# One order list for the whole kernel: the head's loads, transposes and key products move into the program's words

## The chip, the cores and the metric

The kernel runs on one NeuronCore of a Trainium2 chip. Four engines compute: PE (TensorE, matrix products), DVE (VectorE), ACT (ScalarE) and POOL (GpSimd). SP (SyncE) only issues transfers (DMAs); ACT and POOL can issue them too. Each engine works through its own queue in order, and all DMAs are carried out by the same 16 DMA engines. The metric is the device time of one execution in microseconds (us).

## The reference

Tokens S = 2048, width D = 640, 32 attention heads of 20, FFN width 1728, all tensors in bf16.

```
xn  = layernorm(x)                                  # per token, no gain
q,k,v = split(xn @ wqkv)                            # 640 -> 3 x 640
phi(t) = where(t > 0, t + 1, exp(t)) + 1e-6
kv  = sum_s phi(k)_s v_s^T   per head;  z = sum_s phi(k)_s
s   = ((phi(q) @ kv) / (phi(q) . z + 1e-6)) @ wo    # linear attention
g   = silu(relu(xn @ w1) @ w2)                      # FFN, 640 -> 1728 -> 640
out = x + s * g
```

## The kernel before

Tokens are cut into 16 tiles of 128; a tile of x is 128 x 640 bf16, 160 KB. The weights for the keys (wk) are loaded in pieces of 128 rows, 160 KB each; the first FFN weight (w1) in seven column pieces, 320 KB each (the last, piece 6, 240 KB). Most large products use Strassen-like units of seven products each (`unit`, L1159, and `seven`, L1022): the operand sums that they need are made on DVE (L975).

**Recording and order.** Each operation is recorded with what it reads and writes (`Sched`); waits follow from that. `place` then sets the order on each engine from estimated costs. For PE and SP the order is always that of the recording; for ACT, DVE and POOL it is that of the recording up to the call of `end_of_head`, and after it a choice among the next 60 operations of the engine by due times. The recording after the head is driven by a list of words, `PROGRAM`, one word for a step (`a0.s5`: step 5 of unit a0; `n8`: normalise tile 8; `Kb8`: one half of the keys of tile 8).

**The head**, the part that the change touches, was written out as calls in the function body:

- Loads. On the ACT queue x1, x2, x3. On the SP queue x0, wk piece 0, wk piece 1, wk piece 2, wk pieces 3 and 4 in one DMA, w1 pieces 2 and 5, x4, x5, w1 piece 6, x6, x7, w1 pieces 0 and 3 (`x_load` L540, `wk_load` L564, `w1_load` L560).
- Tiles 0 to 3 take a short way to the keys, since their full statistics come late: half of the mean by `bn` on DVE (L635), half or all of it by `mean_act` on ACT (L666), `centre` on DVE (L680, L676), five transposes on PE (L687), copies of the transposed tile out of PSUM by DVE (L697) or ACT (L699), then the key products `K_mm` (L714) in parts by wk piece. `fill` (L603) is a row of products with no use but to keep PE busy: 32 before the first transposes, 3 after those of tile 0. The scale 1/sigma comes later from `aggr` (DVE L639, POOL L641 and L643) and is applied in `K_evac` (ACT L724), which gives exp and relu of the keys.
- Five FFN blocks of the first 512 tokens (`H_block`, PE L804, relu on ACT L808), columns 4, 5, 10, 11, 12, need w1 pieces 2, 2, 5, 5, 6.
- Tiles 4 to 7: statistics on DVE (`LN_stats`), the normalised tile (`LN_norm`, DVE L654), a transposing DMA on the SP queue (L703), then `K_tile` (ten products at L714, and exp and relu). Tiles 0 to 3 are normalised and transposed the same way for later use. `K_fin` (DVE L740, L742) ends the keys of a tile.

After the head come FFN and q products (L1203, L766), the products of keys with x (L1030, L1501), the denominators (L921, L934), and from about 110 us on the FFN's second product and the output (L1030, L1835). The last tile's last 320 columns leave in two pieces (`s_last`), cut by `LC`; each piece has five products (L1835), a product with the gate on DVE, the addition of x on DVE (both L975), and a DMA (L1878).

## Time and profile before

| what | us |
|---|---|
| median of 3 runs (lowest, highest) | 202.2 (202.18, 202.8) |
| span of the profiled execution, first to last instruction | 201.4 |
| PE busy in it | 197.8 |
| DVE busy | 175.1 |
| ACT busy | 130.9 |
| POOL busy | 37.9 |

The span is 0.8 us under the median: the runs' time takes in what lies before the first and after the last instruction, and no time of the profiled execution other than its span was kept. "Busy" is the time in which an instruction of the engine was under way; products on PE overlap, and their ends are modelled. In the rows of the trace a row that merges several instructions gives its start, its length, and in brackets how long the engine had been idle before it and what released it. "PEld" is the loading of a product's stationary operand, "SPq" and "ACTq" are the queues while they issue a DMA.

### The profile page before, as it was taken

The numbers are of one execution on the slowest core, as the hardware profiler recorded it, in microseconds if no ns is written. First come the engines' busy times: TensorE is split into PE (matmuls) and PEld (weight loads), VectorE is DVE, ScalarE is ACT, GpSimd is POOL, SyncE is SP. The second block draws the span as 40 slices with busy tenths as digits, with TensorE's granted clock in tenths as the row PEclk, the third lists the DMA queues.
The fourth block names the chain that finished last, engine by engine and source line by source line (L and its number), as shares of the span: only waits on it lengthen the run. The fifth ranks groups of instructions, "written<-read, shape, count | busy, mean of one in ns | idle before, by whom it ended". The sixth has DMA issues, their size and how long they took to land.

```text
span 201.4 us, 3693 instructions
## 1 busy us (share of the span) xinstructions
PE 197.8 (98%) x1340; PEld 122.6 (61%) x1340; DVE 175.1 (87%) x413; ACT 130.9 (65%) x273; POOL 37.9 (19%) x66
## 2 busy tenths in 40 slices
PE   8999999999999999999999999999999999999995
PEld 7655644455455454445654777777777777767773
DVE  5988999999999888999975999999779786985674
ACT  6598957998999999978653224371555555445643
POOL 3174060363134654152200000000000000000000
PEclk9999999999999999999999999999999999999999
DMA  6977974765545896575910987865961244012103
GB/s 196 326 211 120 264 174 30 189 164 119 116 92 107 163 260 131 102 142 104 245 34 2 324 217 207 263 201 145 373 232 65 68 163 165 0 67 68 65 33 98
DMA packets 38471, 30.43 MB, mean 151 GB/s; under 512 B 13749, under 2 KB 38453, under 8 KB 38453
## 3 DMA queue, kind: packets, MB, share of 16 engines
q1 hardware_dynamic: 32581, 23.28, 41.2%
q0 software_dynamic: 4624, 5.57, 14.3%
q10 hardware_dynamic: 1248, 1.35, 2.1%
q8 instruction: 10, 0.16, 0.3%
q14 instruction: 8, 0.07, 0.1%
HBM read 15.81 MB, written 5.24 MB: 105 GB/s over the span
## 4 chain that ended last, share of the span: by engine, by line
PE 95%; DMA 3%; SPq 1%; DVE 0%; issue 0%; DVEq 0%
PE psT L1030 43%; PE psT L1203 31%; PE psT L714 8%; PE psT L804 5%; DMA reg<-in_A_wqkv_dram 3%; PE psT L1501 2%; PE psT L1835 1%; PE psT L822 1%; PE psT L766 1%; PE psT L1626 1%; PE psT L1600 1%; PE psT L934 1%; DVE reg L975 0%; SPq L564 0%; SPq L540 0%
## 5 line engine op out<-in xcount | busy, mean ns | idle before, releaser
L1203 PE MATMUL psT<-reg 128*128 128x512 bf16 (+2 forms) x159 | 41.7, 370 | 0.0
L1030 PE MATMUL psT<-reg,regH 128*128 128x320 bf16 (+1 forms) x224 | 34.8, 299 | 0.0
L1030 PE MATMUL psT<-reg 128*128 128x320 bf16 (+1 forms) x178 | 29.4, 299 | 0.0
L1030 PEld LDWEIGHTS psT<-reg,regH 128*128 128x128 bf16 (+1 forms) x224 | 21.8, 98 | 8.7 <-DVE psT L975 0.2
L1203 PEld LDWEIGHTS psT<-reg 128*128 128x128 bf16 (+1 forms) x159 | 15.5, 98 | 16.1 <-DVE reg L975 0.7
L902 POOL DMA_DIRECT2D regH<-reg x16 | 18.4, 1238 | 27.0 <-DMA regH<-reg 9.4
L1037 ACT ACTIVATE reg<-psT 128x320 f32<-128x320 f32 (+1 forms) x24 | 10.4, 435 | 17.4 <-PE psT L1030 15.9
L1030 PEld LDWEIGHTS psT<-reg 128*128 128x128 f16 (+1 forms) x178 | 17.3, 98 | 7.2 <-DVE regH L1256 0.4
L975 DVE TENSOR_TENSOR reg<-reg 128x1024 f16<-128x1024 bf16 (+10 forms) x30 | 18.9, 645 | 0.7 <-PE psT L1203 0.6
L1253 ACT ACTIVATE regH<-psT 128x512 bf16<-128x512 f32 (+1 forms) x24 | 14.6, 607 | 4.1 <-PE psT L1203 3.9
L975 DVE TENSOR_TENSOR psT<-psT,reg 128x320 f32<-128x320 f32 (+1 forms) x22 | 11.9, 542 | 5.6 <-PE psT L1030 5.1
L1030 PE MATMUL psT<-reg,pqT 128*128 128x320 bf16 (+1 forms) x84 | 16.3, 299 | 0.0
L1662 ACT ACTIVATE wv_sb<-psT 128x320 bf16<-128x320 f32 (+1 forms) x22 | 9.2, 423 | 10.3 <-PE psT L1030 9.9
L635 DVE BATCH_NORM_STATS2 stats<-reg 128x6 f32<-128x320 bf16 x32 | 13.9, 475 | 1.9 <-DMA reg<-in_A_x_dram 1.9
L1850 ACT ACTIVATE reg<-psT 128x640 bf16<-128x640 f32 (+1 forms) x14 | 8.0, 570 | 9.2 <-PE psT L1030 9.2
L714 PE MATMUL psT<-reg 128*128 128x320 bf16 x80 | 12.3, 299 | 0.0
L1037 ACT ACTIVATE psT<-psT 128x320 f32<-128x320 f32 x17 | 7.3, 427 | 6.8 <-PE psT L1030 6.8
L975 DVE TENSOR_TENSOR reg<-psT,reg 128x320 f32<-128x320 f32 (+2 forms) x19 | 9.5, 504 | 1.4 <-PE psT L1030 1.3
L781 ACT ACTIVATE regE<-psT 128x512 bf16<-128x512 f32 x16 | 9.6, 607 | 1.1 <-PE psT L766 0.5
L714 PEld LDWEIGHTS psT<-reg 128*128 128x128 bf16 x80 | 7.8, 98 | 4.3 <-ACT regH L808 0.3
L643 POOL TENSOR_TENSOR rsy<-rsv,mhalf 128x1 f32<-128x1 f32 x16 | 10.0, 622 | 1.3
L1030 PEld LDWEIGHTS psT<-reg,pqT 128*128 128x128 bf16 (+1 forms) x84 | 8.2, 98 | 3.2
(170 smaller groups left out, 397.9 us busy)
## 6 DMA issues: line engine op xcount, KB each, us to landing
regH<-reg POOLq DMA_DIRECT2D x16, 320.0 KB, 3.7
reg<-in_B_w_dram SPq DMA_DIRECT2D x12, 320.0 KB, 4.6
scr<-rden SPq DMA_DIRECT2D x4, 640.0 KB, 6.7
reg<-in_A_x_dram SPq DMA_DIRECT2D x4, 640.0 KB, 6.3
out_dram<-reg SPq DMA_DIRECT2D x14, 160.0 KB, 1.8
regE<-scr SPq DMA_DIRECT2D x3, 640.0 KB, 5.3
reg<-in_A_x_dram SPq DMA_DIRECT2D x4, 320.0 KB, 3.8
reg<-in_A_wo_dram SPq DMA_DIRECT2D x6, 160.0 KB, 5.0
```

What stands on the lines that cost most here:

```text
L635: sc.op("DVE", lambda eng: eng.bn_stats(stats[:, t, a, :], xv[:, HN * a:HN * (a + 1)]), R=[("xin", xs(t))], W=[("stats", t, a)])
L643: sc.op("POOL", lambda eng: eng.tensor_tensor(out=rsy[:, t:t + 1], in0=rsv[:, t:t + 1], in1=mhalf[:, :], op=ALU.pow), R=[("rsv", t), ("mha ...
L714: fns.append(lambda eng, a=a, k=k, lhs=lhs: eng.matmul(ps[bk[a]][:, 0:HN], lhsT=lhs, rhs=wk[:, k, HN * a:HN * (a + 1)], start=(k == 0), st ...
L781: exps.append(sc.op("ACT", lambda eng: eng.activation(out=e_, in_=src, func=ACTF.Exp), R=[key], W=[("er_e", es)]))
L804: sc.group("PE", [(lambda eng, k=k: eng.matmul(ps[b], lhsT=w1_col(k, P * f, P), rhs=src[:, k, :], start=(k == 0), stop=(k == C - 1))) for ...
L902: dma("POOL", lambda eng: eng.dma_start(zacc[a], src, **kw), R=[key] + after, W=[("zacc", a)], chain=zchain[a])
L975: sc.op("DVE", lambda eng: eng.tensor_tensor(out=out, in0=in0, in1=in1, op=op), R=R, W=W, extra=extra)
L1030: sc.group("PE", [(lambda eng, k=k, lhs=lhs, rhs=rhs: eng.matmul(ps[b][:, 0:HN], lhsT=lhs, rhs=rhs, start=(start and k == 0), stop=(k == n ...
L1037: sc.op("ACT", lambda eng: eng.activation(out=dst, in_=ps[b][:, 0:HN], func=ACTF.Copy), R=[("ps", b)], W=[dkey], extra=extra)
L1203: sc.group("PE", [(lambda eng, k=k, lhs=lhs, rhs=rhs: eng.matmul(ps[b][:, 0:nn], lhsT=lhs if tile is None else rhs, rhs=rhs if tile is Non ...
L1253: sc.op("ACT", lambda eng: eng.activation(out=dst, in_=ps[b], func=ACTF.Relu), R=[("ps", b)], W=[("hT", j, f)], extra=ex)
L1662: sc.op("ACT", lambda eng, lo=lo, hi=hi: eng.activation(out=g[:, lo:hi], in_=src[:, lo - HN * n:hi - HN * n], func=ACTF.Silu), R=[key, ("s ...
```

## The change

The calls of the head are deleted from the function body. `PROGRAM` gets a first part, ending at the word `|`, which says the head in words, so that one list sets the order of everything. What differs from the old head:

- x3 is loaded on the SP queue, no longer on ACT's. wk piece 1 is asked for ahead of piece 0, x3 follows piece 0, and pieces 3 and 4 are two DMAs with x5 between them. x4 stands between w1 pieces 2 and 5, x6 after piece 6, and x7 is the last load, behind w1 pieces 0 and 3.
- On PE the three idle products stay behind the transposes of tile 0, and the transposes of tile 1 come ahead of the first key product. Key products are cut by single wk pieces.
- Copies out of PSUM: the second part of tile 0 goes to ACT, and for tile 2 the parts change engines (DVE now makes four copies, ACT four; before five and three). On DVE the second half of tile 0's statistics stands ahead of the centring of tile 2.
- On ACT the evacuations of the keys of tiles 0 to 3 are interleaved differently, the last pair behind two FFN blocks' relu. The FFN blocks come in the order 4, 10, 5, 12, 11.
- Tiles 0 to 3 are normalised in the order 1, 0 (ahead of the keys of tile 4), 2, 3 (behind those of tile 7).
- The rest of `PROGRAM` holds the same words as before in another order in many places; it starts with block 11 in place of 10.
- `LC` goes from 160 to 192: the last two pieces are 192 and 128 columns wide in place of 160 and 160.

The diff, cut (the new functions only look after which PSUM bank is in use, and call the functions that were called before):

```diff
 PROGRAM = """
-H110 H112 H14 H111 T0 H15 SQ SK xa Q14 a0.s1 a0.s5 Q04 a0.s6 p1.s5 p1.s1 n8 wa xb a0.s2 a0.s7 p1.s6 rb a0.s3 a0.s4
...
+ax1 lx0 ba0 lk12 mh0 lk01 lx3 ax2 ma0 ce0 lk23 lk34 ma1 lx5 lk45 lw2 lx4 lw5 lw6 lx6 ce1 ma2 lw0
+lw3 tr0 pf3 cd0 tr1 cd2 ca1 bb0 lx7 k001 k012 ce2 k102 ca3 ba3 ba2 mh3 ma3 tr2 k123 k023 cd5 ca4 ce3 ag0
+k201 k212 k223 ba1 tr3 k034 cd6 k045 ca7 bb1 k134 k145 k234 ag1 ke0 bb2 kr0 ke1 k245 k301 k312 k324 ag2 S4
+bb3 ke2 k345 kr1 ag3 kr2 P4 P10 ke3 kr3 S5 P5 N4 P12 S6 N5 S7 N6 F0 N7 lx8 F2 lq P11
+F1 F3 N1 N0 KT4 F4 KT5 N2 SH0_1 F5 KT6 KT7 N3 S8 F6 SH0_2 |
+H111 H14 xa F7 H110 H112 SQ Q14 n8 T0 H15 a0.s1 SH0_3 a0.s5 SH0_4 Q04 a0.s6 p1.s5 p1.s1 a0.s2 wa a0.s7 p1.s6 xb
...
-    x_load(0)
-    x_load(1, 1, "ACT")
-    wk_load(0, 1)
-    x_load(2, 1, "ACT")
-    wk_load(1, 2)
-    x_load(3, 1, "ACT")
-    wk_load(2, 3)
-    wk_load(3, 5)
-    w1_load(2, 3, "SP")
-    w1_load(5, 6, "SP")
-    x_load(4)
-    x_load(5)
-    w1_load(6, NW, "SP")
-    x_load(6)
-    x_load(7)
-    for d in (0, 3):
-        w1_load(d, d + 1, "SP")
...
-    bn(0, 0)
-    mean_act(0, HN)
-    half_mean_dve(0)
-    centre(0)
-    mean_act(1, 0)
-    transposes(0, 0)
-    xcT_copy(0, 0, 0, "DVE")
-    centre(1)
-    fill(3)
-    K_mm(0, 2, 0, 1)
-    transposes(1, 6)
-    xcT_copy(0, 0, 1, "DVE")
-    mean_act(2, 0)
-    xcT_copy(1, 6, 0, "DVE")
-    xcT_copy(1, 6, 1, "ACT")
-    K_mm(0, 2, 1, KA)
-    K_mm(1, 4, 0, KA)
-    centre(2)
-    transposes(2, 0)
-    K_mm(0, 2, 2, 3)
...
+    def head_key(t, q, k0, k1):
+        b = (2, 4, 6, 0)[t]
+        assert bank[b] is None if k0 == 0 else bank[b] == ("K", t, k0)
+        bank[b] = bank[b + 1] = ("K", t, k1)
+        K_mm(t, b, k0, k1)
+
+    def head_copy(n, E):
+        t, part = n // 2, n % 2
+        b = (0, 6, 0, 0)[t]
+        assert bank[b + part] == ("T", t, part)
+        xcT_copy(t, b, part, E)
+        bank[b + part] = None
...
-    LC = [0, 160, 320]
+    LC = [0, 192, 320]
...
+        "lx": x_load,
+        "ax": lambda t: x_load(t, 1, "ACT"),
+        "lw": lambda d: w1_load(d, d + 1, "SP"),
+        "ba": lambda t: bn(t, 0),
+        "bb": lambda t: bn(t, 1),
+        "mh": half_mean_dve,
+        "ce": centre,
+        "tr": head_turn,
+        "cd": lambda n: head_copy(n, "DVE"),
+        "ca": lambda n: head_copy(n, "ACT"),
+        "pf": fill,
+        "ag": aggr,
+        "ke": head_exp,
+        "kr": head_relu,
+        "P": head_block,
+        "KT": K_tile,
+        "S": S, "N": N, "F": F,
```

The words read so: `lk12` loads wk piece 1 (rows from 1 up to 2), `k102` makes the key products of tile 1 with wk pieces 0 and 1, `cd5` copies part 1 of tile 2 on DVE (number = 2 x tile + part), `ca4` part 0 of tile 2 on ACT, `ma`, `mh`, `ba`, `bb` are the mean and statistics pieces, `S`, `N`, `F` are `LN_stats`, `LN_norm`, `K_fin`.

More of the change, by code (lines that the diff above doesn't have):

```diff
@@ L1365, in bass_recurrent_scan__linear_attn_block__dense_activation_relu__prompt_kernel, with head_turn, head_exp, head_relu @@
     HP = (4, 5, 10, 11, 12)
-    def K_tile(t, b):
+    bank = [None] * 8
+    copied = set()
+    def head_key(t, q, k0, k1):
[3 more added lines that the diff above has]
+        K_mm(t, b, k0, k1)
+    def head_turn(t):
+        b = (0, 6, 0, 0)[t]
+        for part in range(2):
+            assert bank[b + part] is None
+            bank[b + part] = ("T", t, part)
+        transposes(t, b)
+    def head_copy(n, E):
+        t, part = n // 2, n % 2
+        b = (0, 6, 0, 0)[t]
+        assert bank[b + part] == ("T", t, part)
+        xcT_copy(t, b, part, E)
+        bank[b + part] = None
+    def head_exp(t):
+        b = (2, 4, 6, 0)[t]
+        assert bank[b] == ("K", t, C)
+        K_exp(t, b)
+    def head_relu(t):
+        b = (2, 4, 6, 0)[t]
+        assert bank[b] == ("K", t, C)
+        K_relu(t, b)
+        bank[b] = bank[b + 1] = None
+    def head_block(f):
+        b = RB[ring[0] % len(RB)]
+        assert bank[b] is None
+        H_block(0, f)
+    def K_tile(t):
+        b = 2 * t - 8
+        assert bank[b] is None and bank[b + 1] is None
         K_mm(t, b)
```

83 lines of the change are left out of this document (31 added, 52 removed).

## The prediction

> **What bounds the kernel now.** I read the page first (span, engines, slices), then the chain that ended last, then the head's timeline, then the landings of single DMAs.
>
> ```profile
> span 201.4 us, 3693 instructions
> ...
> PE 197.8 (98%) x1340; PEld 122.6 (61%) x1340; DVE 175.1 (87%) x413; ACT 130.9 (65%) x273; POOL 37.9 (19%) x66
> ...
> PE   8999999999999999999999999999999999999995
> ```
>
> PE is busy all the time but in the first and the last of 40 slices. The chain, in order of time (start, length, what), shows where its row begins:
>
> ```profile
> 2.19 5.20 DMA reg<-in_A_wqkv_dram
> ...
> 7.43 1.53 PE psT L714 x10
> ...
> 9.24 2.99 PE psT L714 x22
> ...
> 17.62 5.47 PE psT L714 x40
> ...
> 132.56 54.22 PE psT L1030 x399
> ...
> 198.33 0.36 PE psT L1835 x5
> ```
>
> From 7.43 to 198.69 us the chain never leaves PE, and its lengths are those of products back to back: 399 products of 128x320 take 54.22 us, 136 ns each, and the 22 at 9.24 take 2.99, 136 ns each too. So the time is 7.43 us until PE's row begins, a fixed sum of products, and 2.7 us behind it. The change adds and removes no product. It can win only what lies ahead of 7.43 or behind 198.7; in between it can only lose.
>
> What PE does until 7.43, with the DVE and ACT work that feeds it:
>
> ```profile
> 4.10 0.64 DVE L680 TENSOR_SCALAR reg<-reg,msum 128x256 bf16<-128x256 bf16 x2
> 5.03 0.38 DVE L676 TENSOR_SCALAR reg<-reg,msum 128x640 bf16<-128x640 bf16 x1
> 5.17 0.45 PE L714 MATMUL psT<-reg,regX 128*128 128x320 bf16 x2
> 5.33 0.76 DVE L697 COPY regX<-psT 128x384 bf16<-128x384 bf16 x2
> 5.47 0.45 PE L687 MATMUL psT<-ident,reg 128*128 128x128 bf16 x5
> 5.76 1.10 PE L714 MATMUL psT<-reg,regX 128*128 128x320 bf16 x6
> 5.96 0.49 ACT L699 ACTIVATE regX<-psT 128x384 bf16<-128x384 bf16 x1 [0.55 <-PE psT L687]
> 6.00 0.38 DVE L676 TENSOR_SCALAR reg<-reg,msum 128x640 bf16<-128x640 bf16 x1
> 6.29 0.88 DVE L635 BATCH_NORM_STATS2 stats<-reg 128x6 f32<-128x320 bf16 x2
> 6.70 0.44 PE L687 MATMUL psT<-ident,reg 128*128 128x128 bf16 x5
> 7.42 1.20 PEld L714 LDWEIGHTS psT<-reg,regX 128*128 128x128 bf16 x10 [0.46 <-DMA reg<-in_A_wqkv_dram]
> ```
>
> By about 7.0 all that tiles 0 to 2 offer with wk pieces 0 and 1 is done, and PE's loading of operands has been idle for 0.46 us when piece 2 lands. That wait is what the head has to give.
>
> **Part 1: the loads, and the wait for wk piece 2.** The chain's DMA row is that piece: issued at 2.19, in at 7.4. The head is limited by transfer; in this row of stages (length, then busy time of PE, PEld, DVE, ACT, POOL, the granted clock, DMA share, GB/s) the DMA engines move 331 GB/s, so a piece of 160 KB (163,840 B) takes 0.49 us:
>
> ```profile
> 7.43:12.07 4.64, 4.64 (x38) 3.42 (x39) 3.83 (x13) 2.97 (x6) 2.36 (x6) 1.00 1.13 331
> ```
>
> Before, piece 2 is the fourth on SP, beside three x tiles on ACT's queue: seven pieces until it is in (x0 to x3, wk 0 to 2). After, it is the fifth on SP, beside two: the same seven, in another mix. So I take no change for piece 2: 7.4 us. Bounds: -0.46 (the wait gone) and +0.49 (one piece more gets ahead of it). That it is issued one DMA later on SP is hidden by the 5.20 us between issue and landing; that piece 1 now comes ahead of piece 0 costs nothing, as both are needed before the wait and come before it.
>
> **Part 2: transposes of tile 1 ahead of the first key product; copies and statistics moved.** On DVE the centring of tile 1 comes ahead of the first copy: it can end at 4.74 + 0.38 = 5.1 in place of 5.41, so PE's transposes of it start at 5.2 (behind the three idle products), not 5.47. The first key products lose their place in that gap and follow at 5.5; their eight (136 ns each) end at 6.6. Tile 2's centring now stands behind the copy that waits for these transposes (to 5.8) and one statistics piece (0.44): it ends at 5.8 + 0.44 + 0.38 = 6.6 against 6.38, and the transposes follow at once, to 6.95. PE is again through at 7.0 and waits for piece 2. Gain 0, loss 0: all of it lies under the wait (gone that cover, 0.2 of tile 2's later centring would be on the path). The regrouped products don't fill the wait: tile 2's with pieces 0 and 1 (`k201 k212`) stand in PE's queue behind `k123`, which needs piece 2. The copy moved to ACT (0.49) takes the place of ACT's 0.55 of idleness. At most the head can give the whole 0.46; next late would then be ACT's copy of tile 2 (from 6.95, 0.49), behind four products of 136 ns, so just covered.
>
> **Part 3: wk pieces 3 and 4 split, x4 to x7 among the w1 pieces.** The old DMA of pieces 3 and 4:
>
> ```profile
> L564 SPq DMA_DIRECT2D reg<-in_A_wqkv_dram x1: 439/439/439, 2.7 to 2.7; - x1
> ...
> DMA to landing us min/median/max: 5.7/5.7/5.7
> ```
>
> In at 2.7 + 5.7 = 8.4, as the ninth piece; piece 4 is now the tenth (x5 ahead), 8.9. It is needed behind tile 3's transposes (to 9.24) and two products (0.27): 9.5. Covered by 0.6; without that cover 0.5. Piece 5 of w1 (for the block of column 10, now second, at 12.2 + 1.1 = 13.3) is moved back behind x4 and x5, 1.0 us; before it was ahead of x4, which was in at 11.0 (row below), so it comes by 12.0. Covered.
>
> DVE's statistics of tiles 4, then 7, and the normalisation of tile 6:
>
> ```profile
> 11.04 0.89 DVE L635 BATCH_NORM_STATS2 stats<-reg 128x6 f32<-128x320 bf16 x2 [0.39 <-DMA reg<-in_A_x_dram]
> ...
> 15.34 0.88 DVE L635 BATCH_NORM_STATS2 stats<-reg 128x6 f32<-128x320 bf16 x2
> ...
> 16.38 0.39 DVE L654 TENSOR_SCALAR reg<-reg,mv,rsy 128x640 bf16<-128x640 bf16 x1
> ```
>
> x4 moves up by one piece, so the 0.39 that DVE waited for it comes back, and tile 7's statistics could begin at 14.95. x7 moves back behind w1 pieces 0 and 3, 640 KB, four pieces, 2.0 us. Its old row:
>
> ```profile
> L540 SPq DMA_DIRECT2D reg<-in_A_x_dram x1: 434/434/434, 8.6 to 8.6; - x1
> ...
> DMA to landing us min/median/max: 4.5/4.5/4.5
> ```
>
> In at 13.1 before, so at 15.1 now: DVE loses 0.15 of its 0.39, PE nothing. But x7 now has the last place in the queue, and the old last load was slow (first rival).
>
> **Part 4: evacuations, FFN blocks, normalisations.** The eight exp and relu of the first four tiles on ACT, and what changes:
>
> ```profile
> 9.82 5.80 ACT L724 ACTIVATE regE<-psT,rsy 128x640 bf16<-128x640 f32 x8
> ```
>
> 0.7 us each. Now two blocks' relu stand ahead of the last two: six from 9.82 end at 14.1, the second relu waits for the block of column 10 (done at 14.4) and ends at about 15, two more: 16.4. The keys of tile 4 need that bank of PSUM at 17.5: covered by 1.1. Tile 3's normalisation moves behind the keys of tile 7; its transposing DMA stands on SP behind the loads of x8 and wq in both kernels, and these hide the delay. Gone that cover, DVE's T0 sums would be late for unit a0.
>
> **Part 5: the rest of the words.** The same operations in another order. A later stage, columns as above:
>
> ```profile
> 30.00:60.00 30.00, 30.00 (x182) 14.60 (x180) 29.74 (x79) 27.82 (x58) 9.52 (x17) 1.00 0.57 115
> ```
>
> No row of before shows the new order. It cannot gain, as PE has no gap there. It can lose: DVE has 0.26 us of idle time in 30, so an operand sum that comes too late stalls PE, by 0.645 for a mean one:
>
> ```profile
> L975 DVE TENSOR_TENSOR reg<-reg 128x1024 f16<-128x1024 bf16 (+10 forms) x30 | 18.9, 645 | 0.7 <-PE psT L1203 0.6
> ```
>
> The nearest row is that of before itself, an order from the same planner without a gap. I take 0, with 1.0 (one sum and a half) as the upper end.
>
> **Part 6: `LC`.**
>
> ```profile
> 198.17 0.86 PE L1835 MATMUL psT<-reg,pqT 128*128 128x160 bf16 x10
> ...
> 198.79 0.67 DVE L975 TENSOR_TENSOR reg<-psT,wv_sb 128x160 bf16<-128x160 f32 x2 [0.22 <-PE psT L1835]
> 199.37 0.38 DVE L975 TENSOR_TENSOR reg<-reg 128x160 bf16<-128x160 bf16 x2
> ```
>
> The ten products keep their sum, so the last ends as before, the first piece 0.07 later. The last piece's gate product (0.67 / 2) and addition (0.38 / 2) lose 32 of 160 columns: at most a fifth of 0.53, 0.1. The first piece's pair grows as much on the same engine, partly beside the last products. I take -0.04; bounds -0.1 and +0.1.
>
> **The sum.** 201.4 (span) + 0 from parts 1 to 5 - 0.04 = 201.36, and 0.8 around it by the median: 202.16. I say 202.1.
>
> **Rivals.** *x7 comes too late (slower).* The place is DVE's queue at tile 7's statistics, which hold tile 6's normalisation behind them. From x7's landing to the end of that: 16.38 - 15.34 + 0.39 = 1.43; tile 6's transposing DMA takes 2.6 more; its keys start at 17.50 + 2 x 1.37 = 20.24 (forty products in 5.47, ten a tile). So x7 must be in by 16.2, and from there each 0.1 later costs PE 0.1. The last two loads of before, w1 pieces 0 and 3, and tile 6's transposing DMA:
>
> ```profile
> L560 SPq DMA_DIRECT2D reg<-in_B_w_dram x2: 433/498/563, 9.1 to 9.6; - x2
> ...
> DMA to landing us min/median/max: 5.0/6.0/7.1
> ...
> L703 SPq DMA_TRANSPOSE reg<-reg x1: 1276/1276/1276, 17.0 to 17.0; - x1
> ...
> DMA to landing us min/median/max: 2.6/2.6/2.6
> ```
>
> The last was in at 9.6 + 7.1 = 16.7, the one ahead of it at 14.1. With x7 at 16.7 the loss is 0.5; issued 0.5 later and as slow, at 17.2, 1.0: 202.6 to 203.1, say 202.9. It decides from 16.8 on (0.6). Beside that last load, from 13.95 to 16.2, a packet of instructions moved, 3.2% of the time of 16 engines, which is half the time of one:
>
> ```profile
> q8 instruction: 1, 0.02, 3.2%
> ```
>
> If that packet held the last load's share of one engine, it would hold x7's now; that speaks for this rival. Against it: 15 engines are untouched, and the sixteenth only matters if it is behind. The Trainium skill, page "Runtime: NRT & Kernel Launch", section "Instruction fetch mechanics", says that an engine's instructions are refilled in blocks of 16 KiB (256 instructions) while the last block runs, at a cost mostly hidden: by that the fetch would return at the same place in PE's stream, which favours this rival's mechanism, but at no cost, which favours the forecast. The trace agrees on the size (0.02 MB in one packet); on the cost it is open.
>
> *The wait for piece 2 shrinks (faster).* With x3 off ACT's queue two queues share the DMA engines for a shorter time, and piece 2 may come up to 0.46 earlier: with part 6, 0.35 to 0.5 less, 201.75. Against it: the bytes ahead are the same.
>
> *The new order stalls PE further down (slower).* Part 5's price, one to one and a half sums: 0.65 to 1.0, 202.9. For it: DVE's 0.26 us of slack. Against it: before is as tight and has no gap.
>
> **How the numbers follow.** The forecast, 202.1 (its own range 201.9 to 202.4): 0.46. Late x7: 0.18, of which 0.13 beyond 0.3%. Shorter wait: 0.21. Worse order: 0.15, of which 0.14 beyond. 0.3% is 0.6 us, about what a measurement of this kernel can tell from no change (the three runs lie that far apart). The shorter wait reaches it only with all of its half microsecond and an earlier x0: 0.08 of its 0.21. So faster 0.08, slower 0.13 + 0.14 = 0.27, the same 0.65. The range goes from 201.6 (all of the wait won, and a little) to 203.1 (late x7 at its upper end).
>
> **What would show it.** Right: the chain begins with the DMA of wk piece 2 and PE's row starts at about 7.4, behind a wait of 0.4 to 0.5 for that load; no idle time of PE after it; last products at 198.7. Wrong by x7: DVE idle ahead of L635 near 15 us, ended by the DMA of x, and PE idle ahead of L714 near 20 us. Wrong by order: gaps of PE after 30 us, ended by DVE L975. Shorter wait: PE's row from about 7.0 on, and all behind it earlier by that.

## The result: slower by 0.55%, and the profile after

The changed kernel takes 203.58 us in the median of 22 runs (202.63 to 205.19), the kernel before, on the same chip, 202.81 (202.18 to 203.53, 22 runs). The ratio of the two is 1.0055, with a 95% interval of 1.0038 to 1.0072: 1.1 us slower (the medians lie 0.77 apart, the means 1.08), outside the predicted range. The runs lie further apart than before, 2.56 us against 1.35.

Lines of the page of the changed kernel, that answer to those of before (201.4 us, PE's first two slices 8 and 9):

```profile
span 203.3 us, 3698 instructions
...
PE 198.4 (98%) x1340; PEld 122.2 (60%) x1340; DVE 173.5 (85%) x412; ACT 130.6 (64%) x274; POOL 38.3 (19%) x66
...
PE   8899999999999999999999999999999999999995
```

Its chain that ended last, in order of time (start, length, what):

```profile
9.79 6.41 DMA reg<-in_A_x_dram
16.23 0.90 DVE stats L635 x2
...
26.65 3.47 DMA reg<-reg
30.15 0.69 DVE regE L917
...
37.58 4.20 DMA reg<-in_A_x_dram
41.80 1.28 DVE stats L635 x3
44.62 2.33 PE psT L1145 x10
...
134.19 47.56 PE psT L972 x350
182.34 6.01 PE psT L972 x43
```

Before, the chain stayed on PE from 7.43 us on. Now it runs through the load of x7 until 16.20, DVE's statistics, a transposing DMA until 30.12, a sum of DVE, another load of x, and joins PE's row for good at 44.62. Even then that row is cut once, at 182. (L917, L972, L1145 and L1819 are the former L975, L1030, L1203 and L1835; L560 and L565 the loads of x and wq, before L540 and L545.)

The stages where PE loses, as window rows (stretch and its length, then busy time of PE, PEld, DVE, ACT, POOL, granted clock, DMA share, GB/s). First the kernel before:

```profile
28.00:31.00 3.00, 3.00 (x16) 1.35 (x14) 3.00 (x7) 2.04 (x5) 0.68 (x3) 1.00 0.40 109
43.00:46.00 3.00, 3.00 (x17) 1.57 (x16) 3.00 (x10) 2.95 (x8) 1.75 (x3) 1.00 0.55 110
178.00:183.00 5.00, 5.00 (x39) 3.49 (x38) 4.01 (x12) 2.36 (x6) 0.00 (x0) 1.00 0.04 13
```

The same stretches of the changed kernel:

```profile
28.00:31.00 3.00, 2.68 (x13) 0.90 (x11) 2.70 (x8) 2.31 (x5) 1.23 (x4) 1.00 0.93 229
43.00:46.00 3.00, 2.67 (x13) 1.06 (x12) 3.00 (x12) 3.00 (x7) 2.35 (x6) 1.00 0.53 139
178.00:183.00 5.00, 4.80 (x36) 3.25 (x35) 3.77 (x13) 1.89 (x4) 0.00 (x0) 1.00 0.19 67
```

A gap is larger than what is missing here, since PE counts as busy until the modelled end of its last product. From start to start of products, less the usual step, PE loses 0.65 us at 29.6 to 30.4 (0.36 and 0.28), 0.49 at 43.9 and 0.36 at 181.8. Another 0.3 is lost ahead of that: PE begins the keys of tile 4 at 17.80, before at 17.50. That is 1.80 us; 0.08 comes back at the end, and 0.09 more is lost at 21.7, in all 1.81. In this execution the span is 1.9 us longer, more than the 1.1 of the ratio: the profiled execution (204.55 us) is one of the slower ones.

### The profile page after: what moved, and what is told of

It reads as the page before. It is cut to its first block, busy times and chain, and to the rows that moved or that the text cites. A ratio compares the mean times of both kernels' runs of the same rounds, so it can differ in the third digit from the quotient of the medians.

```text
span 203.3 us, 3698 instructions
## 1 busy us (share of the span) xinstructions
PE 198.4 (98%) x1340; PEld 122.2 (60%) x1340; DVE 173.5 (85%) x412; ACT 130.6 (64%) x274; POOL 38.3 (19%) x66
## 3 DMA queue, kind: packets, MB, share of 16 engines
q10 hardware_dynamic: 1104, 1.18, 1.7%
## 4 chain that ended last, share of the span: by engine, by line
PE 76%; DVE 8%; DMA 7%; SPq 5%; issue 1%; ACT 1%; POOL 1%; DVEq 0%
PE psT L972 42%; PE psT L1145 25%; DMA reg<-in_A_x_dram 5%; PE psT L714 2%; PE psT L1475 2%; DMA reg<-reg 2%; SPq L560 2%; SPq L580 2%; DVE stats L635 2%; PE psT L1819 1%; PE psT L822 1%; SPq L584 1%; DVE reg L742 1%; ACT regE L724 1%; PE psT L1610 1%
## 5 line engine op out<-in xcount | busy, mean ns | idle before, releaser
L1145 PE MATMUL psT<-reg 128*128 128x512 bf16 (+2 forms) x159 | 41.9, 370 | 0.2 <-DMA reg<-reg 0.2
L972 PE MATMUL psT<-reg,regH 128*128 128x320 bf16 (+1 forms) x224 | 34.7, 299 | 0.2 <-DVE psT L917 0.2
L972 PE MATMUL psT<-reg 128*128 128x320 bf16 (+1 forms) x178 | 28.6, 299 | 0.0
L972 PEld LDWEIGHTS psT<-reg,regH 128*128 128x128 bf16 (+1 forms) x224 | 21.8, 98 | 9.0 <-DVE psT L917 0.5
L1145 PEld LDWEIGHTS psT<-reg 128*128 128x128 bf16 (+1 forms) x159 | 15.3, 98 | 16.5 <-DMA reg<-reg 0.7
L844 POOL DMA_DIRECT2D regH<-reg x16 | 19.0, 1269 | 26.5 <-DMA regH<-reg 13.2
L972 PEld LDWEIGHTS psT<-reg 128*128 128x128 f16 (+1 forms) x178 | 17.3, 98 | 7.2 <-DVE regH L1198 0.4
L917 DVE TENSOR_TENSOR reg<-reg 128x1024 f16<-128x1024 bf16 (+11 forms) x30 | 18.9, 644 | 0.8 <-PE psT L1145 0.6
L635 DVE BATCH_NORM_STATS2 stats<-reg 128x6 f32<-128x320 bf16 x32 | 14.0, 472 | 3.4 <-DMA reg<-in_A_x_dram 3.4
L1646 ACT ACTIVATE wv_sb<-psT 128x320 bf16<-128x320 f32 (+2 forms) x22 | 9.2, 424 | 11.3 <-PE psT L972 11.1
L972 PE MATMUL psT<-reg,pqT 128*128 128x320 bf16 (+1 forms) x84 | 16.5, 299 | 0.0
L917 DVE TENSOR_TENSOR psT<-psT,reg 128x320 f32<-128x320 f32 (+1 forms) x22 | 11.9, 540 | 5.0 <-PE psT L972 3.5
L917 DVE TENSOR_TENSOR reg<-psT,reg 128x320 f32<-128x320 f32 (+2 forms) x19 | 9.5, 502 | 1.2 <-PE psT L972 1.0
L641 POOL TENSOR_SCALAR rsv<-mv 128x1 f32<-128x1 f32 x16 | 4.5, 280 | 30.4 <-DVE mv L639 30.2
```

The lines of the kernel that those rows point to most:

```text
L635: sc.op("DVE", lambda eng: eng.bn_stats(stats[:, t, a, :], xv[:, HN * a:HN * (a + 1)]), R=[("xin", xs(t))], W=[("stats", t, a)])
L844: dma("POOL", lambda eng: eng.dma_start(zacc[a], src, **kw), R=[key] + after, W=[("zacc", a)], chain=zchain[a])
L917: sc.op("DVE", lambda eng: eng.tensor_tensor(out=out, in0=in0, in1=in1, op=op), R=R, W=W, extra=extra)
L972: sc.group("PE", [(lambda eng, k=k, lhs=lhs, rhs=rhs: eng.matmul(ps[b][:, 0:HN], lhsT=lhs, rhs=rhs, start=(start and k == 0), stop=(k == n ...
L1145: sc.group("PE", [(lambda eng, k=k, lhs=lhs, rhs=rhs: eng.matmul(ps[b][:, 0:nn], lhsT=lhs if tile is None else rhs, rhs=rhs if tile is Non ...
L1646: sc.op("ACT", lambda eng, lo=lo, hi=hi: eng.activation(out=g[:, lo:hi], in_=src[:, lo - HN * n:hi - HN * n], func=ACTF.Silu), R=[key, ("s ...
```

## Where the time is lost, in the trace of the changed kernel

*The late load.* DVE's timeline around the statistics of tile 7 (L635) and the normalisations of tiles 6 and 7 (L654):

```profile
16.23 0.89 DVE L635 BATCH_NORM_STATS2 stats<-reg 128x6 f32<-128x320 bf16 x2 [0.99 <-DMA reg<-in_A_x_dram]
...
17.27 0.39 DVE L654 TENSOR_SCALAR reg<-reg,mv,rsy 128x640 bf16<-128x640 bf16 x1
...
18.89 0.45 DVE L654 TENSOR_SCALAR reg<-reg,mv,rsy 128x640 bf16<-128x640 bf16 x1 [0.46 <-POOL rsy L643]
```

x7 is in at 16.20, and tile 7 is normalised at 18.89, before at 18.00. Between 13.7 and 16.2 the same packet of instructions moved as before:

```profile
q8 instruction: 1, 0.02, 2.9%
```

15 of the 16 engines had brought their share of x7 by 14.65, the sixteenth at 16.20. The trace does not number the engines, but the sixteenth must be the one that carried the packet (1.14 us from 13.73): from 14.86 to 15.73, right behind that packet, eight packets of 1280 bytes follow one behind the other, which is one engine's whole share of x7.

*The way to PE.* Timeline of DVE and PE where the first sums of unit a0 (T0) and its first products stand:

```profile
30.15 0.69 DVE L917 TENSOR_TENSOR regE<-reg 128x1024 f16<-128x1024 bf16 x1 [0.30 <-DMA reg<-reg]
30.17 0.60 PE L1145 MATMUL psT<-reg 128*128 128x512 bf16 x2 [0.20 <-DMA reg<-reg]
```

Both wait for the last of the transposing DMAs of tiles 0 to 3. The single landings of SP's queue show the row of which that is the end (the four land one behind the other, some 0.6 us apart; all in us):

| | before | after |
|---|---|---|
| last load of the head in | 16.61 | 16.20 |
| tile 4's transposing DMA in | 17.37 | 16.84 |
| tile 7's transposing DMA in | 21.03 | 21.92 |
| load of x8 issued | 19.71 | 20.61 |
| load of wq in | 25.62 | 26.81 |
| the four of tiles 0 to 3 in | 26.28, 26.86, 27.60, 28.19 | 28.34, 29.00, 29.59, 30.12 |

x7 holds tile 7's normalisation; that holds tile 7's transposing DMA in SP's queue, behind which the loads of x8 and wq are issued, and the four transposing DMAs land only behind wq. At the end of the row 1.93 us are lost. Of these 0.89 are there at tile 7's DMA, 0.30 come with wq, and 0.87 with the first of the four, which lands 1.53 behind wq and not 0.66. That last step isn't x7's: it is as long, 1.52 to 1.59, in five of the eight profiles used below in which x7 is early. Before, the last of the four was in at 28.19, and DVE, busy with other sums, came to it at 28.89: a slack of 0.70.

There is a second way from x7 to T0, through DVE's own queue. Before, T0 and the product that reads it:

```profile
28.89 0.68 DVE L975 TENSOR_TENSOR regE<-reg 128x1024 f16<-128x1024 bf16 x1
29.84 0.59 PE L1203 MATMUL psT<-regE,pqT 128*128 128x512 f16 x2
```

The sum ended 0.27 us ahead of its product. After its wait of 0.99 us for x7 DVE stands idle only once more until T0, 0.46 us at 18.89, as it does before at 18.00. So it can't catch up: it came to T0 at 29.85 (30.15 less the idle 0.30), 0.96 later than before. Had the row on SP been punctual, the sum would have ended at 29.85 + 0.69 = 30.54. PE was ready for the first of these products at 29.81 (30.17 - 0.36) and for the one that reads the sum at 30.24, two products later. By this estimate about 0.3 of the 0.65 us would have been left. So about half hangs on SP's row and half on DVE's own delay.

*The second gap.* T0 is 1.26 us late, and DVE's work behind it as well. So the next tile's transposing DMA is issued 1.25 later (at 34.30, before at 33.05). Its issue then took 2.61 us, before 1.21 (the next packet of PE's instructions moved beside it from 35.10), and the next load of x behind it on SP goes out at 37.58 (35.88 before):

```profile
41.80 1.28 DVE L635 BATCH_NORM_STATS2 stats<-reg 128x6 f32<-128x320 bf16 x3 [0.91 <-DMA reg<-in_A_x_dram]
...
44.62 0.60 PE L1145 MATMUL psT<-regE,reg 128*128 128x512 f16 x2 [0.33 <-DVE regH L917]
```

DVE stands for 0.91 us ahead of these statistics, the sum regH in its queue comes late, and PE waits for that.

## The experiments

The theories named in the expectations: A, x7's last place makes the loss; B, the order of wk pieces 0 and 1 and of x3 in the head costs; C, the new order of the words behind the head has a part of its own; D, what x7 delays is SP's row of transposing DMAs; E, the gap at 181 us is a refill of DVE's instructions; F, PE's packet of instructions holds x7 back. Each ratio is to the kernel before on the same chip.

| run | ratio | 95% interval |
|---|---|---|
| the change | 1.0055 | 1.0038 to 1.0072 |
| x7 up | 1.0006 | 0.9992 to 1.0020 |
| x7 up, again | 1.0019 | 0.9995 to 1.0043 |
| wk piece 0 first | 1.0022 | 1.0008 to 1.0036 |
| old loads | 1.0019 | 0.9998 to 1.0039 |
| before, with x7 last | 1.0017 | 1.0000 to 1.0033 |
| x7 up, piece 0 first | 0.9995 | 0.9979 to 1.0012 |
| old order of the rest | 1.0023 | 1.0005 to 1.0041 |
| PE's instructions later | 1.0058 | 1.0039 to 1.0077 |
| x7 up, piece 0 first, old rest | 0.9987 | 0.9969 to 1.0004 |
| the same, again | 0.9999 | 0.9985 to 1.0014 |
| x7 up, piece 0 first, swap | 1.0014 | 1.0001 to 1.0027 |
| x7 up, swap | 1.0021 | 1.0000 to 1.0042 |
| loads ahead of transposing DMAs | 1.0254 | 1.0222 to 1.0285 |
| all edits | 1.0242 | 1.0211 to 1.0274 |
| DVE's instructions shifted | 1.0042 | 1.0017 to 1.0068 |
| that, x7 up, piece 0 first | 0.9992 | 0.9974 to 1.0009 |

**x7's place.** The changed kernel, with x7 ahead of w1 pieces 0 and 3:

```diff
-... lx6 ce1 ma2 lw0 lw3 tr0 pf3 cd0 tr1 cd2 ca1 bb0 lx7 k001
+... lx6 ce1 ma2 lx7 lw0 lw3 tr0 pf3 cd0 tr1 cd2 ca1 bb0 k001
```

> The changed kernel with one load moved: x7 goes back ahead of w1 pieces 0 and 3 on SP's queue; all else as in the changed kernel. Theory A (x7 as the last load lands at 16.2 us, DVE's queue stands still behind it, tile 7's normalisation, the loads and transposes behind it on SP, and the sums T0 are late, and PE stands still near 29.6, 30.4 and 43.9 us): x7 lands near 13, DVE's wait for it (0.99 us) goes, the two gaps of PE near 30 us (0.36 and 0.28) go, and with them some of the 0.49 near 44; the time falls by 0.6 to 1.1 us against the changed kernel, to a ratio of 0.999 to 1.003 against before. Theory B (the order of wk pieces 0 and 1 and x3 in the head): PE's first key product still starts at about 6.4, the time stays within 0.3 us of the changed kernel's, ratio 1.004 to 1.007. Theory C (the order of the rest of the words): the gaps near 30 us go or not, but those at 43.9 and 181.8 stay; ratio 1.003 to 1.006.

1.0006. The one execution of this run that was profiled has a span of 230.5 us, where the median time is 202.86, so nothing is read from it. The kernel was run again:

> The changed kernel with x7 ahead of w1 pieces 0 and 3 alone, once more, for a profile. Theory A (x7's place is most of the loss): ratio 1.0006 again (1.000 to 1.002), SP's eighth transposing DMA over within 3.9 us of the start of PE's second row of FFN blocks, and no gap of PE at 30 and 44 us; the gap at 181 us stays. Rival (the 1.0006 was a lucky set of runs): 1.003 and more.

1.0019, in a wide interval that holds 1.0006. x7 is in at 12.60, DVE begins its statistics without a wait, wq is in at 25.57 and the last of the four transposing DMAs at 28.00. Two of the windows above, in this run:

```profile
28.00:31.00 3.00, 3.00 (x16) 1.37 (x14) 2.72 (x7) 2.68 (x5) 0.00 (x0) 1.00 0.16 57
43.00:46.00 3.00, 3.00 (x17) 1.54 (x16) 3.00 (x8) 2.89 (x8) 1.26 (x2) 1.00 0.68 135
```

PE is busy throughout; both early gaps are gone, as theory A has it, and the span is 201.2 us. DVE came to T0 at 28.00, 1.85 earlier than in the changed kernel. The gap at 180 us stays. With one place in SP's queue undone most of the loss is gone: 1.0 us by the first run, 0.7 by the second.

**The head's order.** The changed kernel with wk piece 0 ahead of piece 1 (`lk01 mh0 lk12`), and then with the whole old order of the loads. First piece 0:

> The changed kernel with wk piece 0 asked for ahead of piece 1, all else as in the changed kernel. Theory B (piece 0 in second place is what keeps PE waiting until 6.42, 0.4 us later than the work of before at that point): the first key product starts at about 5.5, PE has done the same work about 0.4 us earlier, ratio falls by 0.001 to 0.002 to about 1.004. Rival to B (one slow packet on one DMA engine, which holds whatever load stands there): piece 1 is then late in its place and PE waits for it, first key products with piece 1 at about 6.3; no change in time. Theory A: the gaps near 30 us stay in both cases.

1.0022, less than the 1.004 that theory B expected, and with an interval clear of the change's, though x7 is still last. So x7's place isn't the only one that takes off 0.7 us. The keys of tile 4 begin at 16.93, 0.57 ahead of before, but x7 (in at 16.09) now stops PE in the keys: 0.55 us at 19.5, 0.29 at 21.4, then 0.26 at 29.9. Here the path through tile 6's keys, which the prediction took for the only one, is real, as PE came to it 0.9 us sooner. The 0.26 came by DVE's queue alone: the last of the four transposing DMAs was in at 29.49, and T0 began without a wait.

```profile
29.66 0.68 DVE L917 TENSOR_TENSOR regE<-reg 128x1024 f16<-128x1024 bf16 x1
30.40 0.60 PE L1145 MATMUL psT<-regE,pqT 128*128 128x512 f16 x2
```

With the whole old order of the loads:

> The changed kernel with the whole order of loads of before (x3 on ACT, wk pieces 3 and 4 in one, x4 and x5 behind w1 piece 5, x7 ahead of w1 pieces 0 and 3); products, copies, statistics and the rest of the words as in the changed kernel. If the loads are all of the loss (A and B): ratio 0.998 to 1.001. If the order of the rest has a part of its own (C): gaps of PE at 43.9 (0.49) and 181.8 (0.36) stay, ratio 1.002 to 1.005.

1.0019, just under what theory C expected; of the two gaps that it named the one at 181 us stays, the one at 44 is gone. The old loads in the new order leave 0.40 us of gaps at 29 us: wq in at 26.03, the last of the four at 29.36, and DVE, which came to T0 at 28.87, waited 0.51 for it. So not all of it hangs on x7; the first of the four landed 1.53 us behind wq, as in the changed kernel, and 0.66 behind it before.

**The kernel before, with x7 last.** Only `x_load(7)` is moved behind the loads of w1 pieces 0 and 3:

> The kernel before with one load moved: x7 behind w1 pieces 0 and 3, all else as before. Theory A: x7 lands near 16 us, DVE waits for it about 0.9 us ahead of tile 7's statistics (15.3 in before), tile 7's normalisation and the loads behind it are about 1 us late, and PE stands still between 20 and 35 us for 0.4 to 1.0 us in all: ratio 1.002 to 1.005. Against A: the lateness is taken up by slack in the old order, ratio 0.999 to 1.001.

1.0017, just short of theory A's 1.002 to 1.005. x7 is in at 15.51, 0.7 earlier than in the changed kernel, and PE loses 0.08 us at 21.1 and 0.23 at 29.4. The row on SP was in by 28.35; T0 began at 29.08 without a wait for it, so the 0.23 came by DVE's queue. Its head was 0.36 ahead that time, with the old order in it, the three x tiles on ACT's queue; the lead is given back.

**Both loads, the old rest, and PE's instructions.** First, x7 up and wk piece 0 first:

> The changed kernel with two undone places in SP's queue: wk piece 0 is asked for ahead of piece 1, and x7 ahead of w1 pieces 0 and 3. Theory A with B (x7's lateness makes the loss at 30 and 44 us, wk piece 0 in second place the loss ahead of 7 us): first key product at 5.4 us, keys of tile 4 at about 17.0 (before 17.5), x7 in by 13.0, no gaps of PE at 30 and 44 us; the gap of 0.36 us at 181 us stays. Ratio to before 0.998 to 0.999. Rival (whatever the head gains is given back to DVE before 30 us, as the lead of 0.36 us was when x7 alone was put last in the kernel before): ratio 1.000 to 1.002.

0.9995. The keys of tile 4 at 16.90, no gap at 30 and 44 us, the one at 180 stays: what theory A with B expected of the profile; the ratio is a little above the expected 0.998 to 0.999, which its interval takes in. Next, the changed kernel with the old order of the words behind `|`:

> The changed kernel with the old order of the words behind the head (the new loads and the new head stay). Theory A (the loss up to 45 us comes from x7): the gaps at 30 and 44 us stay, the one at 181 us goes: ratio to before 1.003 to 1.004, against 1.0055 of the changed kernel. Rival 1 (the new order of the rest costs nothing): 1.0055. Rival 2 (the new order of the rest is the whole loss): 1.000.

1.0023, between theory A (1.003 to 1.004) and rival 2 (1.000). Its windows, 28 to 31 first:

```profile
28.00:31.00 3.00, 2.71 (x13) 0.91 (x12) 2.71 (x7) 1.99 (x4) 0.62 (x2) 1.00 0.74 187
43.00:46.00 3.00, 3.00 (x18) 1.54 (x16) 2.96 (x9) 3.00 (x8) 2.02 (x3) 1.00 0.55 109
178.00:183.00 5.00, 5.00 (x39) 3.50 (x37) 4.08 (x13) 1.97 (x4) 0.00 (x0) 1.00 0.02 8
```

The gap at 30 us stays with x7 last (in at 15.59). The one at 181 is gone, and, against the expectation, the one at 44 as well. So the rest of the words does have a part, 0.65 us by the ratios: the old order takes the late T0 without a second gap. With x7 up the new rest has none at 44 either. The parts overlap; their sum is more than the whole.

Third, the 32 idle products of 128 columns ahead of the first transposes as 8 of 512:

```diff
-    fill(32)
+    sc.group("PE", [(lambda eng: eng.matmul(ps[7][:, 0:512], lhsT=one, rhs=wide, start=True, stop=True))
+                    for _ in range(8)], W=[("ps", 7)])
```

> The changed kernel with the 32 idle products of 128 columns ahead of the first transposes made as 8 of 512 columns: the same time of PE, 24 products fewer, so the packet of PE's instructions that moves at 13.7 us should move some 3 us later (24 products of 136 ns). SP's queue is as in the changed kernel, x7 last. Theory F (that packet holds one DMA engine and so x7's share there): x7 in at about 14.7 us in place of 16.2, DVE's wait of 0.99 us for it gone, ratio 1.001 to 1.002. Rival (x7 is late because it is the last in the queue): x7 at 16.2 as before and ratio 1.0055.

The packet moved from 13.73 to 16.79 us, 3.06 later, as worked out, and x7 was in at 14.79. But the ratio is 1.0058. Half of the wait for x7 was left:

```profile
14.81 0.89 DVE L637 BATCH_NORM_STATS2 stats<-reg 128x6 f32<-128x320 bf16 x2 [0.50 <-DMA reg<-in_A_x_dram]
```

(L637 is L635 here.) And the packet now stood beside tile 6's transposing DMA, whose issue on SP took 2.06 us (16.28 to 18.34) where 1.2 to 1.4 is usual: the row on SP was as late as before, wq in at 26.71, the last of the four at 29.18, and PE lost 0.51 us at 29. PE lost another 0.68 us at 123.7, where a weight load on ACT's queue was in 5.5 us after its issue (4.6 at most in the changed kernel); it began again at 124.48. Theory F fits the packet and x7 in this profile (in the six others with x7 last it was in between 15.10 and 16.20), and is wrong on the time. The Trainium skill, page "Runtime: NRT & Kernel Launch", section "Instruction fetch mechanics", has an engine's instructions refilled in blocks of 256; the trace agrees that the place in the stream decides, as 24 products fewer moved the packet by 3.06 us.

Fourth, x7 up, piece 0 first and the old rest:

> The changed kernel with wk piece 0 ahead of piece 1, x7 ahead of w1 pieces 0 and 3, and the old order of the words behind the head; the split of pieces 3 and 4, x3 on SP's queue, the new order of the head's work and the pieces of 192 and 128 columns stay. Theories A, B and C together (each is a part of the loss): no gap at 30, 44 and 181 us, keys of tile 4 at about 17.0, and 0.3 to 0.6 us less than before: ratio 0.997 to 0.9985. Rival (the head's lead is given back to DVE before 30 us): 1.000.

0.9987, and once more:

> The kernel with wk piece 0 first, x7 ahead of w1 pieces 0 and 3, and the old order of the words behind the head (0.9987, interval 0.9969 to 1.0004), once more. If the head's lead reaches the end: 0.998 to 0.999 again. Rival (the kernel's time is that of before within what can be measured): 1.000 to 1.001.

0.9999. Neither is told from the kernel before. In both profiles no gap of PE is left at 30, 44 or 181 us (there is a new one of 0.16 at 58), and the spans are 201.5 and 201.4. But the keys of tile 4 begin at 17.51 and 17.30, not at the 17.0 that was expected (before 17.50): in these two executions the head had little or no lead to keep.

**The gap at 181 us.** Its rows in the changed kernel:

```profile
181.78 0.50 DVE L917 TENSOR_TENSOR psT<-psT,reg 128x320 f32<-128x320 f32 x1 [1.18 <-PE psT L972]
...
182.34 6.01 PE psT L972 x43
```

(The second is the chain's.) I first read it as a matter of two words, o4.s7 ahead of o4.s3, and swapped them, with x7 up, with and without wk piece 0 first:

> The changed kernel with wk piece 0 ahead of piece 1, x7 ahead of w1 pieces 0 and 3, and, near the end, o4.s3 ahead of o4.s7 as in the kernel before. Theory C (DVE's sum behind o4.s3, 0.50 us, is covered by the four products of o4.s7 where these follow, and by one product where they do not): the gap of 0.36 us at 180 us goes, all else as without the swap (which gave 0.9995): ratio 0.9977, faster than the kernel before. Rival (the time won there is lost again before the end): 0.9995.

> The changed kernel with x7 ahead of w1 pieces 0 and 3 and the swap of o4.s3 and o4.s7; wk piece 1 stays ahead of piece 0. Theory B (piece 0 in second place costs the head 0.3 us and more): the first key product later than 5.6 us, ratio 0.9988, that is 0.001 above the kernel that has piece 0 first as well. Rival (the late piece 0 of the profiled execution was one slow packet and not its place): as that kernel, 0.9977.

The gap stayed, 0.36 us in both: that reading was wrong. The ratios, 1.0014 and 1.0021, are not those expected. Both profiles have a gap ahead of the keys of tile 4 (0.46 and 0.44 us at 16.6): the last load of the head was in at 16.37 and 16.07, tile 4's transposing DMA landed behind it at 17.09 and 17.18. The second has 1.12 us at 29 as well, with wq in at 26.79. The gap in the first:

```profile
17.23 0.97 PE L714 MATMUL psT<-reg 128*128 128x320 bf16 x6 [0.30 <-DMA reg<-reg]
```

On wk: the first key product comes at 5.49 with piece 1 first and at 5.38 with piece 0 first, and the ratios lie within each other's intervals, so theory B has no support here; for it speaks only the run with piece 0 alone moved, 1.0022. The 6.42 of the changed kernel's profile was piece 0 in at 6.28, by one packet of 1.09 us on one engine; in six other profiles with piece 1 first it was in at 5.2 to 5.5.

Then DVE's first memset was cut into seven parts, so that all of DVE's later instructions stand six places further on; the order of every engine is unchanged:

```diff
-    sc.op("DVE", lambda eng: eng.memset(hT[:, NF, :], 0.0), W=[("hz",)])
+    sc.group("DVE", [(lambda eng, c=c: eng.memset(hT[:, NF, 256 * c:256 * (c + 1 if c < 6 else 8)], 0.0))
+                     for c in range(7)], W=[("hz",)])
```

> The changed kernel with DVE's first memset cut into seven parts (the same elements; DVE is idle there), so that all later instructions of DVE stand six places further on in its stream; the order of every engine is as in the changed kernel. Theory E (the gap of 0.36 us at 181 us is a refill of DVE's instructions: its sum starts 0.40 us after the wait ahead of it has ended, 0.04 elsewhere, and a packet of DVE's instructions moves 0.9 us later): the gap goes, ratio 1.0037 against 1.0055. Rival (it belongs to the order of the words there): the gap stays, ratio 1.0055.

> As the run before, in the kernel with wk piece 0 first and x7 ahead of w1 pieces 0 and 3 (0.9995 without the shift): by theory E no gap of PE at 180 us and ratio 0.998; by the rival 0.9995 with the gap.

The gap is gone in both. The same sum in the first:

```profile
179.44 0.50 DVE L918 TENSOR_TENSOR psT<-psT,reg 128x320 f32<-128x320 f32 x1 [0.83 <-PE psT L973]
```

It starts 0.83 us after DVE's last work, not 1.18, and the packet of 8 KB, which in the changed kernel began 0.94 us behind the sum (182.72 against 181.78), now begins at 177.53, 1.9 ahead of it. Counted in DVE's records, the sum is number 448 in all eight profiles with the gap; in those without it, it is number 446 or 447 (the old order), 449 (the two runs on SP's row below) or 454 (the shift). So the 0.36 us belongs to DVE's place in its stream of instructions, not to the words. That it is the fetch of the next instructions is inferred from the packet beside it. The Trainium skill, page "Runtime: NRT & Kernel Launch", section "Instruction fetch mechanics", calls the crossing of a block of instructions mostly hidden. The changed kernel has eight such packets of 8 KB, and PE has a gap of this kind beside this one alone; here, with PE waiting for DVE, the runs show 0.36 us. The ratio is 1.0042 for the shift alone (1.0037 expected) and 0.9992 with the two loads moved (0.998).

The first of these profiles shows more. x7 is still last, but the laggard engine was quick: x7 in at 15.10, the last of the four transposing DMAs at 28.42, no gap at 30 or 44, and a span of 201.0 us, less than before. The twelve runs of that kernel go from 202.21 to 204.81. So a kernel with x7 last is not slow in every execution. Its time seems to hang on when one engine has finished; the runs that were only timed don't show it.

**SP's row.** x7 stays last, but SP issues the loads of x8 and wq while it waits:

```diff
-... P12 S6 N5 S7 N6 F0 N7 lx8 F2 lq P11 F1 F3 N1 N0 KT4 ...
+... P12 S6 N5 S7 lx8 lq N6 F0 N7 F2 P11 N1 N0 F1 F3 KT4 ...
```

> The changed kernel with x7 last as it is, but SP's queue filled while it waits for x7: the loads of x8 and wq are issued ahead of tile 6's transposing DMA (they were behind tile 7's), and the normalisations of tiles 1 and 0 stand ahead of the two sums F1 and F3 on DVE. Theory D (what x7's lateness really delays is SP's row of eight transposing DMAs, whose last sets when T0's sums can begin; PE stalls when that last one ends more than 9.3 us after the keys of tile 4 begin): that end comes at about 26.5 in place of 27.9 us, the gaps at 30 and 44 us go with x7 still last, ratio 1.002 to 1.003 (the head and the gap at 181 us remain). Rival (x7 delays PE through the keys of tiles 6 and 7, as the prediction had it): gaps and ratio as in the changed kernel, 1.0055.

1.0254, five us slower; neither theory had it. The last issue of the row on SP ended at 26.20, as worked out, and there is no gap at 30. But PE stood still before:

```profile
22.97 1.37 PE L714 MATMUL psT<-reg 128*128 128x320 bf16 x5 [2.68 <-DMA reg<-reg]
```

Tile 6's transposing DMA was issued by 18.55 and landed at 22.92, 0.65 behind wq (22.27). In the changed kernel, with no load ahead of it, it was issued by 18.90 and landed at 20.27. A transposing DMA lands behind the bytes of the loads issued ahead of it, and 1.1 MB takes longer than the wait that I filled. The stop isn't all: behind it, from 22.97 to 27.00, the granted clock was 0.58 in the profiled execution. The twenty products there took 4.40 us, at 136 ns each 2.72, so 1.7 us more were lost, and 0.84 at 44 us. T0 began only at 30.55 in that execution, though the last transposing DMA was in at 27.57, so the run can't decide on theory D. The last run has this edit with all the others:

> The changed kernel with all of the edits that helped: wk piece 0 first, x7 ahead of w1 pieces 0 and 3, the swap of o4.s3 and o4.s7, and the loads of x8 and wq ahead of tile 6's transposing DMA with the normalisations of tiles 1 and 0 ahead of F1 and F3. Theory D (SP's row has slack once x7 is early): the last edit changes nothing, ratio 0.997 to 0.998, as without it. Rival (in other executions than the profiled one a late load still runs through SP's row into PE): lower by 0.001 or more.

1.0242: the same stop, 3.11 us at 19.6, this time with a granted clock of 1.00 behind it. It says nothing more on SP's slack.

## Why the prediction was wrong

The forecast was 202.1 by a sum of nothing but -0.04, with "late x7" as a rival at 0.18. The failing step is in part 3; the sum's last term was off as well, apart from the change. It put 0.8 us around the span, but in the runs on record the time of a profiled execution is 1.24 to 1.28 above its span (204.55 for 203.31 in the changed kernel). With 1.25 the same sum gives 202.6, and the kernel before measured 202.81. So about 0.45 of the 1.5 us between 202.1 and 203.58 is not the change.

**Part 1, the loads.** The wait for wk piece 2 did not stay. Piece 2 was in at 7.07, in the run with x7 up at 6.40, and between 6.02 and 7.07 in all fourteen profiles with x3 on SP's queue that are used here. That is what the rival *shorter wait* said. That the move of x3 did it isn't shown: with x3 on ACT's queue piece 2 was in at 7.38, 7.22 and, in the kernel before with x7 last, 6.43. Nor is a gain shown at the end: in the profiles with x7 up the keys of tile 4 begin between 16.90 and 17.51, before at 17.50, and in the kernel before with x7 last at 17.14. In the profile where neither x7 nor DVE's refill got in the way the span is 0.4 us shorter than before, but the ratios don't show it (0.9987 to 1.0021 with x7 up). A reason against it is in the profiles: tile 4's transposing DMA lands 0.6 us or more behind the last load of the head, and in three of them, where it was in at 17.1 to 17.2, PE stood for 0.26 to 0.46 us ahead of those keys. "That piece 1 comes ahead of piece 0 costs nothing" held but for one execution, the profiled one.

**Part 2, tile 1's transposes.** No run took it apart, so its zero isn't shown. In the timeline of the change nothing but the load stands ahead of the first key product:

```profile
6.38 0.94 PEld L714 LDWEIGHTS psT<-reg,regX 128*128 128x128 bf16 x8 [1.07 <-DVE reg L676]
6.42 1.25 PE L714 MATMUL psT<-reg,regX 128*128 128x320 bf16 x8 [0.93 <-DVE reg L676]
```

The profile names DVE's centring as the releaser, but that had ended at 6.34 and belongs to tile 2; piece 0 was in at 6.28.

**Part 3, x7: the step that failed.** "In at 15.1: DVE loses 0.15 of its 0.39, PE nothing." The size was off: x7 was in at 16.20 in the profile (between 14.8 and 16.2 where it was last), and DVE lost 0.99. But the true error was the path. I followed x7 to the keys of tile 6, which gave a limit of 16.2. Two tighter ways lead to T0. One is DVE's own queue, which had 0.27 us of slack there (part 5 itself had found 0.26 us of idle time in 30); the wait of 0.99 came out at T0 as 0.96. The other goes through tile 7: its transposing DMA, x8, wq, the four transposing DMAs behind wq, T0. At its end was 0.70 us of slack, and 1.93 were lost, 0.89 of it by x7. "PE nothing" became 0.65 us at T0 and 0.49 at 44 us. The rows for both ways were in the trace of before; I had read them as hiding a delay.

**Part 4.** "Its transposing DMA stands on SP behind the loads of x8 and wq, and these hide the delay": these loads came late themselves and were part of the delay. I named the consequence (T0 late for a0) and looked for its cause only in tile 3's normalisation.

**Part 5, the order of the rest.** Taken as 0, bound 1.0. Undoing it gave 0.65 us (1.0055 to 1.0023), inside the bound. But its price was not a sum that comes too late by its place. One half answers to x7's lateness (44 us), the other to where DVE's instructions are refilled (181 us).

**Part 6, `LC`.** -0.04 predicted. The last ten products and the last additions:

```profile
200.15 0.85 PE L1819 MATMUL psT<-reg,pqT 128*128 128x192 bf16 x10
...
201.30 0.38 DVE L917 TENSOR_TENSOR reg<-reg 128x192 bf16<-128x192 bf16 x2
```

From the first of these products to the end of the span it is 203.3 - 200.15 = 3.15 us, before 201.4 - 198.17 = 3.23: -0.08, inside the bounds.

**The rivals.** *Late x7* was right in its place (DVE's queue at L635), in the packet beside the load and in its price, 0.5 to 1.0 (moving x7 up gave 0.7 and 1.0). The price is luck: on the rival's own way, through the keys of tile 6, x7 at 16.20 costs nothing. It had too little chance, since I let 15 punctual engines speak against it. *Worse order* was right on size, by another mechanism, and so by luck.

Open: what the place of wk piece 0 gave in the one run where it was moved alone (1.0022 against 1.0055; the landings differ too much from execution to execution to tell); why the first transposing DMA behind wq lands 0.6 to 0.7 us after it in some profiles and 1.5 in others; and what a kernel with both early gaps removed gains for certain. None of these kernels is told from the kernel before as faster; the best two readings are of one kernel, 0.9987 and 0.9999.

## What to carry to other kernels

A load that is moved back must be followed through every queue behind its consumer to the place with the least slack, not only to the first product that needs it: here DVE's own queue had 0.27 us of slack and a row of DMAs on SP 0.70, and the load cost DVE 0.99. A load is in when the slowest of its 16 engines is done, and x7, last in the queue, was in 1.55 us behind the other fifteen; so don't put there what the critical path needs first. When a small gap appears far from any edit, shift the instruction stream by a few places before blaming the order.

## What the runs showed of the hardware

- A transposing DMA landed behind all loads issued ahead of it on SP's queue: 0.6 to 1.6 us behind the last load of the head and behind wq, and the three that follow wq's first 0.5 to 0.8 apart. Moving 1.1 MB of loads ahead of one made it land 4.4 us after its issue had ended, in place of 1.4.
- One packet of 16 KB of PE's instructions took 1.0 to 1.2 us on one DMA engine in the head (0.9 to 1.8 later in the changed kernel). The share of the last load on that engine came 1.6 us behind the other fifteen (2.2 in the kernel before). Where the packet began within the issue of a transposing DMA (at 13.35, 13.38 and 16.79 us in three runs), that issue took 1.85, 1.86 and 2.06 us, not 1.2 to 1.4. The next packet shows the same near 34 us: in nine profiles it began 0.6 to 0.82 us into the issue of a transposing DMA, and that issue took 2.0 to 2.6 us; in four it began 0.86 us into it or later, and there the issue took 1.2 to 1.4 and the one behind it 1.1 to 1.5, where 0.6 is usual. But one of the four behind wq takes as long in most profiles with no such packet beside it.
- At one place of DVE's instruction stream an operation began 0.35 us late, and PE, which waited for it, lost 0.36; six places further on in the stream the delay was gone.
- After PE had stood still for 2.8 us, the granted clock was 0.58 for the next 4 us in one profiled execution; after 3.1 us in another it stayed at 1.00.
